# An S5 scan gated by a GeGLU feed-forward: token-major norm, one-pass GELU, pair-wide rotations and a fixed TensorE order

## The chip, the cores and the metric

The kernel runs on one core of a Trainium2 chip. The metric is the device time of one execution in microseconds (us). Every time below is a median of several executions. All are of the fast state, but for three executions of one kernel (c7), which are named. "Span" is the length of the one execution that was profiled; the times lie 1.6 to 1.9 us above it. Engines are called by the profile's names: PE is TensorE (PEld its weight loads), DVE is VectorE, ACT is ScalarE, POOL is GpSimd, SP is the engine that issues most transfers; a "q" behind a name is that engine's queue of DMA issues.

## The reference, cut to what matters

```python
x  = A_x                                    # (1, 2048, 512), bf16
xn = (x - mean(x)) / sqrt(var(x) + 1e-5)
# diagonal complex recurrence of 512 states
Lam_bar = exp(dt * Lam);  B_bar = ((Lam_bar - 1) / Lam)[:, None] * (B_re + 1j * B_im)
h[t] = Lam_bar * h[t-1] + B_bar @ xn[t]
s  = 2 * real(h @ (C_re + 1j * C_im).T) + xn * Dskip
# gate
g  = silu((gelu(xn @ w_gate) * (xn @ w_up)) @ w_down)        # 512 -> 1376 -> 512
out = x + s * g
```

The sequence is worked on in four slabs of 512 tokens. The complex recurrence becomes a real one by a rotation: the inputs are turned by a cosine and sine table, two real scans run with the factor |Lam_bar|, and the result is turned back.

## The kernel before

Three parts matter. The norm is channel-major: PE sums with a matrix of ones, ACT takes logarithm and exponential for 1/sqrt, and PE can do nothing else until it is through. The GELU has three ACT passes and two extra VectorE operations per tile:

```python
nc.scalar.activation(out=zb[:fs], in_=g_ps[:fs, :], func=AF.Copy)
nc.scalar.activation(out=sq[:fs], in_=g_ps[:fs, :], func=AF.Square, scale=math.sqrt(A_GELU))
nc.vector.scalar_tensor_tensor(out=arg[:fs], in0=sq[:fs], scalar=1.0, in1=zb[:fs], op0=ALU.add, op1=ALU.mult)
nc.scalar.activation(out=sg[:fs], in_=arg[:fs], func=AF.Sigmoid, scale=2.0 * C_GELU)
# ... up projection, Copy to ub; then zu = zb * ub and at = sg * zu on VectorE
```

The rotations work on one block of 128 states at a time: twelve `tensor_tensor` of 512 columns and two scans per block (cut):

```python
nc.vector.tensor_tensor(out=p1[:], in0=ure[:], in1=cos_b[:, pt, :], op=ALU.mult)
nc.vector.tensor_tensor(out=p2[:], in0=uim[:], in1=sin_b[:, pt, :], op=ALU.mult)
nc.vector.tensor_tensor(out=wre[:], in0=p1[:], in1=p2[:], op=ALU.add)
# ... the same for wim, two scans, carries, and six more to turn back
```

## Time and profile before

| before | value | how to read it |
|---|---|---|
| time | 266.82 us (266.12 to 267.13, 4 runs) | slowest core; there is one |
| span | 265.3 us | the profiled execution |
| busy PE / DVE / ACT | 195.9 / 228.3 / 157.4 us | sums of durations; they count overlap of pipelined work too |
| longest PE wait | 16.3 us, for the GELU's Square | ends at 58.59 us, where the body begins |

### The profile page before, as it was taken

The page shows a single profiled execution, that of the slowest core. Times are in us where ns is not written, and L with a number is a line of the kernel's source. Part 1 is how long each engine was busy: PE and PEld are TensorE (multiplying, and loading weights), DVE is VectorE, ACT ScalarE, POOL GpSimd, SP SyncE. Part 2 cuts the span into 40 slices and gives each one's busy share as a digit, 9 for nine tenths or more (in the row PEclk, how much of TensorE's full clock was granted, in tenths as well). Part 3 has the DMA queues.
Part 4 walks back from the last instruction along what each step waited for, and adds up shares of the span by engine and source line. Part 5 has one row for each costly group of instructions (what it writes and reads, how often), then busy time and mean ns, then how long its engine had stood idle before and what let it go on. Part 6 is the DMA issues. An engine that isn't in the chain of part 4 may idle for free.

```text
span 265.3 us, 2923 instructions
## 1 busy us (share of the span) xinstructions
PE 195.9 (74%) x863; PEld 86.3 (33%) x880; DVE 228.3 (86%) x600; ACT 157.4 (59%) x279; POOL 1.0 (0%) x8
## 2 busy tenths in 40 slices
PE   0045663019979889797795998789889788978993
PEld 0011221003434334343341443334444333434451
DVE  0405999987999999999999899999999999998243
ACT  0219999438747759748577527758475757922410
POOL 1000000000000000000000000000000000000000
PEclk9999759556999999999997999999999999999999
DMA  8999548100000000000000310000013000002201
GB/s 79 259 251 252 99 100 250 61 0 1 4 0 0 0 0 2 0 1 0 0 4 0 99 59 1 2 0 0 0 46 115 1 1 0 2 0 79 79 22 61
DMA packets 26224, 12.81 MB, mean 48 GB/s; under 512 B 19712, under 2 KB 25184, under 8 KB 26208
## 3 DMA queue, kind: packets, MB, share of 16 engines
q1 hardware_dynamic: 21520, 10.17, 15.8%
q10 hardware_dynamic: 4688, 2.46, 4.1%
q8 instruction: 7, 0.11, 0.2%
q14 instruction: 9, 0.07, 0.1%
HBM read 6.33 MB, written 2.10 MB: 32 GB/s over the span
## 4 chain that ended last, share of the span: by engine, by line
DVE 67%; PE 11%; ACT 9%; DMA 5%; issue 4%; SPq 2%; ACTq 1%; DVEq 0%
DVE fim L362 7%; DVE fre L359 7%; DVE arg L409 7%; DVE at L423 5%; DVE zu L422 5%; DMA xT<-in_A_x_dram 5%; PE y_ps L450 5%; PE f_ps L434 4%; DVE p L343 2%; DVE p L348 2%; DVE wre L344 2%; DVE p L349 2%; DVE hst L388 2%; DVE q L392 2%; DVE q L387 2%
## 5 line engine op out<-in xcount | busy, mean ns | idle before, releaser
L401 PE MATMUL g_ps<-xnT,wg 128*128 128x512 bf16 (+1 forms) x171 | 48.4, 399 | 32.7 <-ACT sq L407 28.5
L416 PE MATMUL u_ps<-xnT,wu 128*128 128x512 bf16 (+1 forms) x173 | 47.8, 396 | 6.3 <-ACT uim L338 5.9
L413 ACT ACTIVATE sg<-arg 128x512 bf16<-128x512 bf16 (+1 forms) x44 | 28.0, 636 | 34.0 <-DVE arg L409 34.0
L434 PE MATMUL f_ps<-wd,at 128*128 128x512 bf16 (+1 forms) x174 | 42.5, 379 | 3.5 <-ACT sf L440 2.2
L405 ACT ACTIVATE zb<-g_ps 128x512 bf16<-128x512 f32 (+1 forms) x44 | 26.6, 605 | 26.5 <-DVE zu L422 17.1
L401 PEld LDWEIGHTS <-wg 128*128 128x128 bf16 (+1 forms) x176 | 18.0, 103 | 53.0 <-issue 36.5
L450 PE MATMUL y_ps<-C,hst 128*128 128x512 bf16 x126 | 31.3, 379 | 1.3 <-DVE yg L462 0.8
L409 DVE SCALAR_TENSOR_TENSOR arg<-sq,zb 128x512 bf16<-128x512 bf16 (+1 forms) x44 | 29.9, 679 | 1.2 <-ACT sq L407 1.2
L416 PEld LDWEIGHTS <-wu 128*128 128x128 bf16 (+1 forms) x176 | 18.3, 104 | 29.6 <-issue 11.9
L420 ACT ACTIVATE ub<-u_ps 128x512 bf16<-128x512 f32 (+1 forms) x44 | 27.2, 618 | 0.0
L407 ACT ACTIVATE sq<-g_ps 128x512 bf16<-128x512 f32 (+1 forms) x44 | 26.8, 609 | 0.0
L434 PEld LDWEIGHTS <-at 128*128 128x128 bf16 (+1 forms) x176 | 17.0, 98 | 24.7 <-DVE at L423 2.3
L275 PE MATMUL mean_ps<-xT,onesK 128*128 128x512 bf16 x16 | 6.7, 563 | 19.1 <-DMA xT<-in_A_x_dram 17.2
L423 DVE TENSOR_TENSOR at<-sg,zu 128x512 bf16<-128x512 bf16 (+1 forms) x44 | 18.5, 421 | 1.5 <-ACT sg L413 1.5
L422 DVE TENSOR_TENSOR zu<-zb,ub 128x512 bf16<-128x512 bf16 (+1 forms) x44 | 18.4, 419 | 0.0
L462 DVE TENSOR_TENSOR yg<-y_ps,g 128x512 bf16<-128x512 f32 x16 | 10.7, 683 | 8.1 <-PE y_ps L454 7.8
L450 PEld LDWEIGHTS <-hst 128*128 128x128 bf16 x128 | 12.2, 98 | 14.9 <-issue 1.0
L325 PE MATMUL u_re_ps<-xnT,BreT 128*128 128x512 bf16 x62 | 16.1, 378 | 0.2
L331 PE MATMUL u_im_ps<-xnT,BimT 128*128 128x512 bf16 x61 | 16.1, 379 | 0.2
L438 ACT ACTIVATE fb<-f_ps 128x512 f32<-128x512 f32 x16 | 9.8, 613 | 9.7 <-PE f_ps L434 9.4
L359 DVE TENSOR_TENSOR_SCAN fre<-rho,init_re,wre 128x512 bf16<-128x512 f32 x12 | 15.3, 1279 | 0.0
L362 DVE TENSOR_TENSOR_SCAN fim<-rho,init_im,wim 128x512 bf16<-128x512 f32 x12 | 15.3, 1279 | 0.0
(119 smaller groups left out, 264.9 us busy)
## 6 DMA issues: line engine op xcount, KB each, us to landing
xres<-in_A_x_dram SPq DMA_DIRECT2D x16, 128.0 KB, 2.2
out_dram<-ot SPq DMA_DIRECT2D x16, 128.0 KB, 1.7
wu<-in_B_w_up_dram ACTq DMA_DIRECT2D x1, 1376.0 KB, 6.8
wg<-in_B_w_gate_dram SPq DMA_DIRECT2D x1, 1376.0 KB, 8.0
wd<-in_B_w_down_dram SPq DMA_DIRECT2D x1, 1280.0 KB, 6.9
wd<-in_B_w_down_dram SPq DMA_DIRECT2D x1, 96.0 KB, 6.6
BreT<-in_A_B_re_dram SPq DMA_TRANSPOSE x4, 6.0
BimT<-in_A_B_im_dram SPq DMA_TRANSPOSE x4, 2.7
```

Of the source, the lines that this page charges most:

```text
L359: nc.vector.tensor_tensor_scan(out=fre[:], data0=rho_b_ap, data1=wre[:], initial=ire, op0=ALU.mult, op1=ALU.add)
L362: nc.vector.tensor_tensor_scan(out=fim[:], data0=rho_b_ap, data1=wim[:], initial=iim, op0=ALU.mult, op1=ALU.add)
L401: nc.tensor.matmul(g_ps[:fs, :], lhsT=wg[:, kt, fsl], rhs=xnT[:, kt, cols], start=(kt == 0), stop=(kt == KT - 1))
L407: nc.scalar.activation(out=sq[:fs], in_=g_ps[:fs, :], func=AF.Square, scale=math.sqrt(A_GELU))
L409: nc.vector.scalar_tensor_tensor(out=arg[:fs], in0=sq[:fs], scalar=1.0, in1=zb[:fs], op0=ALU.add, op1=ALU.mult)
L413: nc.scalar.activation(out=sg[:fs], in_=arg[:fs], func=AF.Sigmoid, scale=2.0 * C_GELU)
L416: nc.tensor.matmul(u_ps[:fs, :], lhsT=wu[:, kt, fsl], rhs=xnT[:, kt, cols], start=(kt == 0), stop=(kt == KT - 1))
L420: nc.scalar.activation(out=ub[:fs], in_=u_ps[:fs, :], func=AF.Copy)
L422: nc.vector.tensor_tensor(out=zu[:fs], in0=zb[:fs], in1=ub[:fs], op=ALU.mult)
L423: nc.vector.tensor_tensor(out=at[:fs, j, :], in0=sg[:fs], in1=zu[:fs], op=ALU.mult)
L434: nc.tensor.matmul(f_ps[:, :], lhsT=at[:fs, k, m0 : m0 + P], rhs=wd[:fs, k, :], start=(k == 0), stop=(k == NFT - 1))
L450: nc.tensor.matmul(y_ps[:, :], lhsT=hst[:, j, m0 : m0 + P], rhs=C2[:, j, :], start=(j == 0), stop=False)
```

## The change

The intent: take work from VectorE until PE is the bound, and shorten the start. The diff cut to its core (cuts marked):

```diff
-  nc.scalar.activation(out=zb[:fs], in_=g_ps[:fs, :], func=AF.Copy)          # and sq, arg, sg, zu
+  nc.scalar.activation(out=gt[:fs], in_=g_ps[:fs, :], func=AF.Gelu_apprx_tanh)
+  nc.scalar.activation(out=ub[:fs], in_=u_ps[:fs, :], func=AF.Copy)
+  with tc.high_priority():
+      nc.vector.tensor_tensor(out=at[:fs, j, :], in0=gt[:fs], in1=ub[:fs], op=ALU.mult)
...
+  # norm on token-major tiles: bn_stats, bn_aggr, power on GpSimd, one tensor_scalar,
+  # then PE transposes (slab 0) or DMA transposes (slabs 1 to 3)
...
+  # rotation of a pair of blocks at once: 2 x 2048 columns and 2 x 1024
+  nc.vector.tensor_tensor(out=pp[:], in0=src[:], in1=cb, op=ALU.mult)
+  nc.vector.tensor_tensor(out=qq[:], in0=src[:], in1=sinp[:, :, hs, :], op=ALU.mult)
+  nc.vector.tensor_tensor(out=dst0, in0=pp[:, 0, :, :], in1=qq[:, 1, :, :], op=op)
+  nc.vector.tensor_tensor(out=dst1, in0=pp[:, 1, :, :], in1=qq[:, 0, :, :], op=op)
...
+  # cosine and sine tables by two long Sin passes; the input factor folded into C:
+  nc.scalar.activation(out=tA[:], in_=CT[:, 1, pt, :], func=AF.Copy, scale=cim[:, pt : pt + 1])
+  nc.vector.scalar_tensor_tensor(out=C2[:, 0, pt, :], in0=CT[:, 0, pt, :], scalar=cre[:, pt : pt + 1],
+                                 in1=tA[:], op0=ALU.mult, op1=ALU.subtract)
...
+  # silu by tanh, so that gate and GELU need no change of table set
+  nc.scalar.activation(out=th[:], in_=f_ps[:, :], func=AF.Tanh, scale=0.5)
+  nc.vector.scalar_tensor_tensor(out=g2[:], in0=th[:], scalar=1.0, in1=f_ps[:, :], op0=ALU.add, op1=ALU.mult)
...
+  # PE, ACT, SP and GpSimd keep the order of the program; VectorE's order is left to the compiler.
+  for s in range(NS):
+      # slab 0: FFN tiles first (with the fold of C on tiles 3 to 6), then the input matmuls, norms of 2 and 3
+      # later slabs: input matmuls, then FFN tiles, with the output y of slab s-1 after tiles 4, 6, 8, 10
+      # then the four down projections of slab s
```

## The prediction

> **What bounds the kernel now.** I read the page's busy row and slices first, then the busy time by stretches, the timeline of VectorE (DVE), the timeline of TensorE (PE), and the sums of waits.
>
> Parts 1 and 2 of the page, busy time and the 40 slices of 6.6 us:
>
> ```profile
> PE 195.9 (74%) x863; PEld 86.3 (33%) x880; DVE 228.3 (86%) x600; ACT 157.4 (59%) x279; POOL 1.0 (0%) x8
> ...
> PE   0045663019979889797795998789889788978993
> ...
> DVE  0405999987999999999999899999999999998243
> ```
>
> VectorE is full from slice 5 to slice 37; PE has work from slice 9 on and is not full. The busy time in three stretches, cut where the first and the last slab's feed-forward work lies (columns: stretch, its length, then busy us and instructions of PE, PEld, DVE, ACT, POOL):
>
> ```profile
> 0.00:57.40 57.40, 17.93 (x48) 6.20 (x49) 38.00 (x148) 31.10 (x38) 0.98 (x8) 0.82 0.72 156
> 57.40:245.00 187.60, 162.15 (x733) 72.63 (x748) 182.65 (x439) 121.94 (x233) 0.00 (x0) 0.97 0.05 15
> 245.00:265.30 20.30, 15.78 (x84) 7.52 (x84) 7.67 (x14) 4.34 (x8) 0.00 (x0) 1.00 0.16 53
> ```
>
> So there are three parts: a prologue of 57.4 us in which PE gets 48 matmuls, a body of 187.6 us in which DVE is busy for 97%, and a tail of 20 us that PE alone fills. A mean duration hides overlap, so I take costs from the distance between starts. In the VectorE timeline of the steady state (start, us, operation):
>
> ```profile
> 101.26 0.68 DVE L409 SCALAR_TENSOR_TENSOR arg<-sq,zb 128x512 bf16<-128x512 bf16 x1
> 101.89 0.42 DVE L423 TENSOR_TENSOR at<-sg,zu 96x512 bf16<-96x512 bf16 x1
> 102.23 0.41 DVE L422 TENSOR_TENSOR zu<-zb,ub 128x512 bf16<-128x512 bf16 x1
> 102.57 0.41 DVE L342 TENSOR_TENSOR p<-ure,cos_b 128x512 bf16<-128x512 bf16 x1
> ...
> 104.58 1.27 DVE L359 TENSOR_TENSOR_SCAN fre<-rho,init_re,wre 128x512 bf16<-128x512 f32 x1
> 105.77 0.39 DVE L350 TENSOR_TENSOR wim<-p,p 128x512 bf16<-128x512 bf16 x1
> ```
>
> A bf16 tensor_tensor of 512 columns costs 0.335 us (101.89 to 102.23 to 102.57), a scalar_tensor_tensor 0.60 to 0.63, a scan 1.19. The same distances in the table stage give 0.20 for 256 columns and 0.60 for 1024, so I extrapolate 1.13 us for 2048. Check, per slab: 11 feed-forward tiles x (0.60 + 0.335 + 0.335) = 14.0; four scan blocks x (12 x 0.335 + 2 x 1.19 + 0.4 for the carries) = 27.2; the gate and output work 4 x (0.60 + 0.60 + 0.335) = 6.1; together 47.3, and four slabs are 189 against the 187.6 of the body. VectorE's work is the body.
>
> The PE timeline where PE has no wait (start, us, operation and count):
>
> ```profile
> 105.11 1.03 PE L401 MATMUL g_ps<-xnT,wg 128*128 128x512 bf16 x4
> 105.98 1.03 PE L416 MATMUL u_ps<-xnT,wu 128*128 128x512 bf16 x4
> 106.84 1.03 PE L401 MATMUL g_ps<-xnT,wg 128*128 128x512 bf16 x4
> ```
>
> Four matmuls take 0.865 us, 0.2163 each, not the 0.379 to 0.401 of the groups. And in the sums of waits (total, times, longest), PE's waits stand behind the three-pass gelu:
>
> ```profile
> ACT sg L413 <- DVE arg L409: 34.0, 20, 4.2
> PE g_ps L401 <- ACT sq L407: 28.5, 12, 16.3
> ```
>
> **What the Trainium skill says.** (1) "TensorE: Matmul & The Clock Gate", section "Back-to-back issue gap": a warm matmul of N columns follows the last after N/2.4 + 2.5 ns, 216 for 512; this trace has 216.3. (2) The same page, Part 1: PE runs at half clock until some 3.4 us of activity, and again after an idle window. The body's granted clock of 0.97 and the prologue's 0.82 agree. (3) "VectorE: DVE Perf Modes", section "The perf-mode tier table": bf16 tensor_tensor in SBUF reaches 2x, single-source operations 4x in bf16 and 2x in fp32, PSUM sources less. The 0.335 us for 512 columns is 256 cycles plus about 0.07, so 2x is seen here; 4x on 512 columns is not seen here. (4) "ScalarE: Activation LUTs", section "What ACT_TABLE_LOAD costs": 1283 ns for a change of set; this trace has eleven loads of 1283 ns, eight of them in the old norm.
>
> **The change, part by part.**
> *Feed-forward.* The scalar_tensor_tensor and one tensor_tensor of each tile go: -0.94 us x 44 = -41 us of VectorE. ScalarE falls from four passes to two, about 0.49 us each by its starts, 1.0 us a tile beside 8 x 0.2163 = 1.73 of PE: PE no longer waits there.
> *Rotations.* One rotation over a pair of blocks costs 2 x 1.13 (2048 columns) + 2 x 0.60 (1024) = 3.46 instead of 2 x 6 x 0.335 = 4.02; a slab has four (two pairs, before and after the scan): 13.9 instead of 16.1. The scans stay, 8 x 1.19 = 9.5; carries about 1.0. With 11 x 0.335 = 3.7 for the gated product and 6.1 for the gate and output, VectorE needs 34.2 us a slab instead of 47.3.
> *PE a slab.* 196 matmuls of 512 (32 input, 88 feed-forward, 44 down, 32 output) x 0.2163 = 42.4, and 16 skip matmuls x 0.055 = 0.9: 43.3 us. That is above VectorE's 34.2, so **PE becomes the bound of the body**, and its total, 4 x 43.3 = 173.1 us, is what must be laid down. The old ones-matmuls of the norm go.
> *Prologue.* The order is fixed, so I walk it. Parameters land at about 5.5 (four issues of 0.5 us from 0.73, then 2 us), exp and two products until 6.8; statistics 4 x 0.6 + 0.6 (an estimate at one element a cycle) and the power on POOL until 10.5; four norms, PE transposes, four copies: xnT of slab 0 at 13.6 and PE starts. Then VectorE's tables: eight fp32 angle passes of 0.33 to 0.6, two fp32 passes over 2056 columns of 2.2 (2056 / 0.96 GHz), until 21 to 23; ScalarE's cosine takes 1.9 (as its 2048-column Square did), the small sines and a table load follow, and only then comes the first gelu, at 25 to 27, since ScalarE keeps program order. PE has by then done two tiles (16 matmuls) and stands with its four PSUM buffers full. **PE restarts at 26.5.** VectorE meanwhile does the coefficients (3.4) and the norm of slab 1 (5) and reaches the first gated product at 33; four buffers of gelu output and four of PSUM carry PE to about 35, so this costs little.
> *Stream.* 768 x 0.2163 + 3.5 = 169.6.
> *Losses on it.* Cold clock after the idle 2; folding C puts two ScalarE copies of about 0.7 on four tiles, where 2.4 exceeds 1.73: 2.6; slab 0's state against its first reader: VectorE from 33 has 46 us of work (norms of slabs 2 and 3 at 5 each, fold 5, products 5, gate 2.4, chains 24), so it is ready at 79, and PE wants it at 79: 2; other short waits 4.
> *Tail.* Output and skip matmuls, product, add, store: before, the last matmul ended at 260.9 of 265.3: 4.4.
> Sum: 26.5 + 169.6 + 2 + 2.6 + 2 + 4 + 4.4 = 211.1 us of span; times lie 1.6 above the span (266.9 against 265.3): **212 to 213 us**.
>
> **The rivals.**
> *A: VectorE stays the bound.* The cosine operand is now repeated by an outer step of zero. If that, or the four-dimensional pattern, loses the 2x rate in all four operations, a rotation costs about 6.7, a slab's four go from 13.9 to 27 and VectorE to 47, above PE's 43: 4 x 4 = 16 us more, about 228. For it: nothing in this trace has such an operand in a tensor_tensor. Against: the inner run is still dense, and the copies with a repeated inner element ran at 2x (1024 columns in 0.60).
> *B: the start costs more.* The norms of slabs 2 and 3 have high priority and their inputs arrive early, while VectorE's order in the body is left to the compiler. If they come before the first gated products, these move from 33 to 43 and PE, which can run to 35, stands for 8 us: about 220. For it: the page shows the first 57 us already lost to serial start-up. Against: VectorE has nothing else to do before slab 0's inputs arrive.
> *C: no start-up stall.* If the tables finish while PE still has free PSUM, PE runs through from 14: about 203. Against: ScalarE's two long sines alone take 3.8 us and wait for 4.4 us of fp32 passes.
> *D: late state.* If slab 0's state comes 10 us later than I count, PE waits as long at the first output matmul, about 220, and the clock drops for some us after.
>
> **Range and chances.** A and B each have perhaps one chance in six, C one in ten; most of the error is above the middle, as waits only add. I take 212, with 203 to 226. Even rival A with B, near 236, is 11% faster, and nothing I see costs 55 us. Faster 0.97, within 2% 0.02, slower 0.01.
>
> **What would show each step right or wrong.** Right: PE's slices at 9 from slice 6 on with few waits; VectorE's busy time near 185 us and gaps in the body; starts of the 2048-column rotations 1.13 apart; the first gated product near 33 us and the first gelu near 26; output matmuls that do not wait for the state. Wrong: rotations 2.2 apart (A); PE idle for over 5 us between 28 and 45 (B); a long PE wait for hst in slab 1 (D); the gelu and tanh taking turns of table loads between single tiles.

## The result, and the profile after

The changed kernel takes **227.01 us** (225.93 to 227.62, 4 runs) against 266.82: a ratio of 0.8503, 95% interval 0.8465 to 0.8541, faster. Ratios here are the mean time of one kernel's fast runs over that of the other's of the same rounds, so not quite the ratio of the medians. The direction was right; the time lies 1 us above the predicted range and 15 us above the predicted value.

The busy row and the slices of the page after (40 slices of 5.6 us):

```profile
PE 183.6 (82%) x849; PEld 84.6 (38%) x865; DVE 173.4 (77%) x315; ACT 95.1 (42%) x156; POOL 6.4 (3%) x13
...
PE   0018939069966999999829999999999999999993
...
DVE  1079869966899899999994279999932999995443
```

PE is full from slice 22 on (counted from 1), where the prediction had slice 6; before that it has holes. VectorE is full in the middle. The busy time in three stretches (columns as in the prediction: stretch, length, then busy us and instructions of PE, PEld, DVE, ACT, POOL, then granted clock):

```profile
18.60:60.00 41.40, 30.44 (x117) 12.79 (x119) 32.94 (x93) 27.87 (x45) 3.54 (x3) 0.88 0.55 122
60.00:117.00 57.00, 48.04 (x221) 21.83 (x224) 56.03 (x85) 21.14 (x36) 0.00 (x0) 0.94 0.06 14
117.00:220.00 103.00, 102.53 (x494) 48.01 (x502) 76.61 (x116) 43.06 (x72) 0.00 (x0) 0.98 0.04 15
```

From 117 us on PE is the bound, to within half a microsecond of 103. From 60 to 117 us VectorE is full, with 56.03 of 57.00; whether by the amount of its work or by its order is what the experiments ask. The prediction's "PE becomes the bound of the body" holds for the second half only.

PE's longest stops in its timeline (start of the work after the stop; in brackets the stop and what ended it):

```profile
31.39 1.54 PE L335 MATMUL up_ps<-xnT,wu 128*128 128x512 bf16 x4 [3.41 <-ACT ub L341]
45.90 1.87 PE L330 MATMUL g_ps<-xnT,wg 128*128 128x512 bf16 x4 [6.32 <-ACT gt L339]
68.93 6.60 PE L350 MATMUL f_ps<-wd,at 128*128 128x512 bf16 x22 [3.74 <-DVE g L357]
115.29 0.61 PE L350 MATMUL f_ps<-wd,at 128*128 128x512 bf16 x1 [4.11 <-DVE at L343]
```

With three shorter stops (0.37, 0.70 and 0.84) they make 19.5 us. After most of them the next matmuls are slow: the 22 after 68.93 took 6.60 us where 22 x 0.2163 is 4.76. From PE's start at 18.65 to its last matmul's end at 220.3 are 201.65 us; the whole stream at full rate is 4 x 43.3 = 173.1. So 28.5 us are lost, 19.5 in stops and 9 in slow matmuls and small gaps; of these 9, 1.4 come at PE's very start (eight matmuls in 3.12 us from 18.65).

Where the stops come from. The one at 45.90 is ACT waiting to fold C (ACT timeline):

```profile
41.20 0.72 ACT L257 ACTIVATE tA<-CT,cim 128x512 f32<-128x512 bf16 x1 [3.07 <-issue]
44.64 0.72 ACT L258 ACTIVATE tB<-CT,cim 128x512 f32<-128x512 bf16 x1 [2.71 <-DVE C L263]
45.27 0.58 ACT L339 ACTIVATE gt<-g_ps 128x512 bf16<-128x512 f32 x1
```

The fold's scratch has two buffers, and VectorE frees them late, because between 34.1 and 43.8 us it is mostly busy with the batch statistics of slabs 1 to 3. ACT keeps its order, so the GELU of the next tile stands behind the fold. The stops at 68.93 and 115.29 are VectorE's order (VectorE timeline, two pieces):

```profile
59.93 1.21 DVE L292 TENSOR_TENSOR pp<-U,cos_b 128x2048 bf16<-128x2048 bf16 x1
61.06 1.21 DVE L293 TENSOR_TENSOR qq<-U,sinp 128x2048 bf16<-128x2048 bf16 x1
...
63.52 4.56 DVE L306 TENSOR_TENSOR_SCAN Ft<-rho,Wt 128x512 bf16<-128x512 f32 x4
...
68.20 0.68 DVE L357 SCALAR_TENSOR_TENSOR g<-th,f_ps 128x512 f32<-128x512 f32 x1
...
110.10 2.46 DVE L306 TENSOR_TENSOR_SCAN Ft<-rho,it,Wt 128x512 bf16<-128x512 f32 x2
...
114.80 0.43 DVE L343 TENSOR_TENSOR at<-gt,ub 128x512 bf16<-128x512 bf16 x1
```

The gate at 68.20, which frees a down projection's PSUM bank, stands behind four scans, and the gated product at 114.80 behind two scans, an output product and a rotation, though ACT had delivered its inputs by 108 us. The first two lines show something else: the 2048-column rotations start 1.13 us apart (59.93 to 61.06), as extrapolated. Rival A is refuted.

The start (ACT timeline, queue of DMA issues and engine):

```profile
9.06 0.41 ACTq L88 DMA_DIRECT2D wu<-in_B_w_up_dram  x1
9.50 1.28 ACT L119 ACT_TABLE_LOAD   x1 [9.50 <-DMA wu<-in_B_w_up_dram]
10.79 0.21 ACT L119 ACTIVATE dt__124<-pf 128x4 f32<-128x4 f32 x1
```

The parameters had landed at 5.6 us, but the exponential stands behind six weight issues on ACT's queue, the last of which went out at 9.06. So PE began at 18.65 and not at 13.6.

### The profile page after: what moved, and what is told of

It reads as the page before. It is cut to its first block, busy times and chain, and to the rows that moved or that the text cites. A ratio compares the mean times of both kernels' runs of the same rounds, so it can differ in the third digit from the quotient of the medians.

```text
span 224.2 us, 2436 instructions
## 1 busy us (share of the span) xinstructions
PE 183.6 (82%) x849; PEld 84.6 (38%) x865; DVE 173.4 (77%) x315; ACT 95.1 (42%) x156; POOL 6.4 (3%) x13
## 4 chain that ended last, share of the span: by engine, by line
PE 49%; DVE 36%; DMA 8%; ACT 4%; POOL 1%; issue 1%; SPq 0%; DVEq 0%; POOLq 0%
PE f_ps L350 13%; PE g_ps L330 10%; PE up_ps L335 9%; PE y_ps L367 9%; DVE Ft L306 8%; PE u_ps L280 6%; DVE st L136 4%; DVE pp L292 4%; DVE qq L293 4%; DMA xnT<-xn 4%; DVE at L343 3%; DMA wu<-in_B_w_up_dram 2%; DMA pv<-in_A_log_dt_dram 2%; DVE xn L147 2%; PE y_ps L372 1%; POOL rs L142 1%
## 5 line engine op out<-in xcount | busy, mean ns | idle before, releaser
L335 PE MATMUL up_ps<-xnT,wu 128*128 128x512 bf16 (+1 forms) x174 | 46.8, 391 | 3.5 <-ACT ub L341 3.4
L339 ACT ACTIVATE gt<-g_ps 128x512 bf16<-128x512 f32 (+1 forms) x44 | 26.3, 597 | 33.8 <-PE g_ps L330 33.4
L341 ACT ACTIVATE ub<-up_ps 128x512 bf16<-128x512 f32 (+1 forms) x44 | 26.3, 598 | 11.8 <-PE up_ps L335 11.4
L306 DVE TENSOR_TENSOR_SCAN Ft<-rho,it,Wt 128x512 bf16<-128x512 f32 x24 | 29.6, 1273 | 0.0
L280 PE MATMUL u_ps<-xnT,BT 128*128 128x512 bf16 x124 | 28.1, 379 | 0.2
L357 DVE SCALAR_TENSOR_TENSOR g<-th,f_ps 128x512 f32<-128x512 f32 x16 | 11.0, 686 | 19.1 <-ACT th L354 19.1
L284 ACT ACTIVATE U<-u_ps 128x512 bf16<-128x512 f32 x32 | 19.1, 598 | 8.2 <-PE u_ps L280 8.2
L280 PEld LDWEIGHTS <-BT 128*128 128x128 bf16 x128 | 12.5, 98 | 15.1
L343 DVE TENSOR_TENSOR at<-gt,ub 128x512 bf16<-128x512 bf16 (+1 forms) x44 | 18.0, 416 | 0.0
L136 DVE BATCH_NORM_STATS2 st<-x_tok 128x6 f32<-128x512 bf16 x16 | 10.1, 684 | 0.0
```

The costliest lines, as they stand in the source:

```text
L136: nc.vector.bn_stats(out=st[:, m, :], in_=x_tok[:, s * M + m, :])
L280: nc.tensor.matmul(u_ps[:, :], lhsT=BT[:, ri, kt, pt * P : (pt + 1) * P], rhs=xnT[:, kt, cols], start=(kt == 0), stop=(kt == KT - 1),)
L284: nc.scalar.activation(out=U[:, ri, q, :], in_=u_ps[:, :], func=AF.Copy)
L306: nc.vector.tensor_tensor_scan(out=Ft[:, ri, q, :], data0=rho[:, pt : pt + 1].to_broadcast([P, TS]), data1=Wt[:, ri, q, :], initial=init, ...
L335: nc.tensor.matmul(u_ps[:fs, :], lhsT=wu[:, kt, fsl], rhs=xnT[:, kt, cols], start=(kt == 0), stop=(kt == KT - 1))
L339: nc.scalar.activation(out=gt[:fs], in_=g_ps[:fs, :], func=AF.Gelu_apprx_tanh)
```

## The experiments

Two theories stood at the outset, and the texts use these names. **Load**: VectorE has too much work before 117 us (tables, norms, fold, chains of slabs 0 and 1), and PE's stops are where that surfaces; a stop taken away comes back elsewhere. **Order**: the stops are separate accidents of the instruction order, and each one mended pays in full. A "chain" is rotation, scans, and rotation back of a pair of blocks. They ran in six calls, each on one chip and beside runs of the kernel before (medians 266.74 to 267.11); the chips differ between most calls (c4, c5 and c8 shared one, c6 had another), so times are compared across chips.

| run | us, median (range) | ratio to before, 95% | span |
|---|---|---|---|
| changed kernel | 227.01 (225.93–227.62) | 0.8503 [0.8465, 0.8541] | 224.2 |
| e1_fold4 | 225.37 (224.35–225.95) | 0.8425 [0.8372, 0.8478] | 224.2 |
| e2_norm_late | 222.54 (221.38–223.12) | 0.8326 [0.8280, 0.8373] | 219.6 |
| e3_exp_early | 223.70 (223.30–225.85) | 0.8392 [0.8336, 0.8448] | 221.4 |
| e4_rot_single | 231.22 (229.87–232.05) | 0.8652 [0.8601, 0.8703] | 228.1 |
| e5_gelu3 | 259.67 (257.55–260.97) | 0.9710 [0.9650, 0.9770] | 257.6 |
| e6_stats_shared (wrong on purpose) | 220.25 (219.23–220.67) | 0.8237 [0.8201, 0.8273] | 218.5 |
| e7_y_same | 252.04 (251.21–252.50) | 0.9429 [0.9382, 0.9475] | 250.2 |
| c2_combined | 221.01 (220.44–221.50) | 0.8270 [0.8237, 0.8304] | 219.4 |
| c4_uncoupled | 211.52 (211.35–212.87) | 0.7941 [0.7907, 0.7975] | 209.5 |
| c5_no_u_ahead | 211.21 (210.78–211.35) | 0.7911 [0.7892, 0.7930] | 209.5 |
| c6_weights_act | 219.85 (218.79–220.86) | 0.8249 [0.8203, 0.8295] | 217.4 |
| c7_dve_order | one fast run 213.43, three slow 217.11–218.68 | none | 216.9 (slow) |
| c8_dve_even | **206.98** (205.17–207.55) | 0.7750 [0.7694, 0.7806] | 204.9 |

### e1: the fold's stop taken away

```diff
-  tA = work.tile([P, D], FP32, name="tA", tag="tA")              # 2 buffers; tB alike
+  tA = work.tile([P, D], BF16, name="tA", tag="tA", bufs=4)
```

> The scratch of the folding of C gets four buffers instead of two (as bf16, for space). In the changed kernel TensorE stands 6.3 us at 39.4 us because ScalarE waits for this scratch. Theory 'order' (the three stalls are accidents of VectorE's order): this stall and about 1.6 us of cold clock after it go, 218 to 221 us. Theory 'load' (VectorE has too much to do before 117 us, and a stall that is taken away comes back at the gate or at the gated products): 225 to 228 us, with longer waits of TensorE at 65 and at 111 us.

The stop at 45.90 went (0.30 us is left there), and nearly all of it came back (PE timeline):

```profile
65.59 6.72 PE L350 MATMUL f_ps<-wd,at 128*128 128x512 bf16 x22 [5.76 <-DVE g L357]
...
113.09 4.46 PE L350 MATMUL f_ps<-wd,at 96*128 96x512 bf16 x12 [2.30 <-DVE at L343]
```

The gate's stop grew from 3.74 to 5.76, and a second gate stop of 1.98 us came; the two stops at the products are 2.04 and 2.30, where they were 4.11 and 0.84. The gain is 1.6 us, which is not clear of the noise: the intervals of the two ratios overlap, and both profiled spans are 224.2. As load said: PE came sooner to a VectorE that was not sooner.

### e2: the norms of slabs 2 and 3 a slab later

```diff
-            ln_dma(2)                    # after slab 0's input matmuls, at high priority
-            ln_dma(3)
+                if j == 0 and s < NS - 1:
+                    ln_dma(s + 1)        # in the slab before its use, without priority
```

> The norms of slabs 2 and 3 lose their high priority and are emitted one slab later (11 us of VectorE work, most of it moved behind the first slab's gated products). Theory 'load': the work moves towards the half in which VectorE has slack, so 217 to 220 us. Theory 'order': the stall at the fold goes as well, since nothing stands in front of the fold any more, so again 218 to 221; this run tells both from a third, that the early weight of the norms is harmless: 226 to 228.

222.54: the direction is right, the gain of 4.5 us is smaller than both theories said. The compiler still placed a part of the statistics early, and stops of 2.4, 2.0, 3.5 and 2.7 us remain.

### e3: the exponential ahead of four weight issues

```diff
+    nc.scalar.activation(out=rho[:], in_=a1[:], func=AF.Exp)
+    # weight loads 3 to 6 are issued here, after both exponentials, not before them
```

> The two exponentials of the parameters are issued on ScalarE ahead of the last four weight loads instead of behind all six. Expected: the first exponential at about 6.3 us instead of 10.8, TensorE's first feed-forward matmul at about 14.2 instead of 18.65. If VectorE's work bounds the time until 117 us ('load'), everything after it moves with it: 222 to 223 us. If the start is bound by the weights or by the transposed loads behind it, 226 to 227.

PE started at 13.80, 4.85 us sooner, and 3.3 us arrived at the end; 223.70 is 0.7 above what load said. The blocked queue had only moved: now the first GELU stood behind the last weight issue (ACT timeline):

```profile
18.87 0.52 ACTq L131 DMA_DIRECT2D wu<-in_B_w_up_dram  x1
19.42 1.28 ACT L343 ACT_TABLE_LOAD   x1 [12.84 <-DMA BT<-in_A_B_im_dram]
```

### e4: the pair-wide rotations undone

```diff
-        nc.vector.tensor_tensor(out=pp[:], in0=src[:], in1=cb, op=ALU.mult)     # 2048 columns
+        for q in range(H2):                                                     # 512 columns each
+            for ri in range(2):
+                TT(out=pp[:, ri, q, :], in0=src[:, ri, q, :], in1=cos_b[:, pt, :], op=ALU.mult)
```

> The pair-wide rotations are undone: 12 operations of 512 columns instead of 4 of 2048 and 1024, all else as in the changed kernel. VectorE gets 16 x 0.56 = 9 us more. If VectorE bounds nothing: 227. If it bounds the first two of four slabs only ('load'): half of it, 230 to 233. If it bounded the whole body: 236.

VectorE's busy time rose from 173.4 to 181.3, and the time by 4.2 us, about half. (PE also started later, at 19.89 for 18.65, which the edit does not explain.) That fits a kernel that VectorE bounds in its first half and PE in its second.

### e5: the three-pass GELU back

```diff
-        nc.scalar.activation(out=gt[:fs], in_=g_ps[:fs, :], func=AF.Gelu_apprx_tanh)
+        # Copy, Square, arg = (sq + 1) * zb, Sigmoid one tile later, zu = zb * ub, at = sg * zu
```

> The three-pass gelu of the kernel before goes back into the changed kernel (its last sigmoid, product and product a tile later, so that ScalarE's fixed order doesn't wait for VectorE): VectorE gets 44 x 0.94 = 41 us more and its work per slab, about 44.5 us, passes TensorE's 43.3. 'Load': VectorE then bounds the whole body, its busy sum of about 173 becomes 214 and the time 245 to 258 us. If the one-pass gelu mattered only in the first two slabs (half of 41): about 247 at most, and with VectorE idle in the second half; if it mattered little because TensorE bounds: below 235.

259.67, a little above the range. VectorE's busy time rose by 40.7 us to 214.1 (the prediction's term for this is 41). So 32.7 us of the 39.8 us that the change gains hang on this part.

### e6: the norm's statistics of slabs 1 to 3 left out (a wrong result on purpose)

```diff
-            mv, rs = ln_stats(s)
+            mv, rs = mv0, rs0            # slab 0's statistics; relative error 0.123
```

> Wrong result on purpose: slabs 1 to 3 are normalised with slab 0's mean and scale, so 12 batch statistics and 12 aggregates of VectorE, about 8.7 us, all before 60 us, are gone and nothing else moves. 'Load': the waits of TensorE at the fold, the gate and the gated product shrink by about as much in sum: 217 to 220 us. 'Order' without load: only the wait at the fold (6.3 and 1.6 of cold clock) changes: 219 to 221, with the waits at 65 and 111 us as they were. If neither: 226 to 228.

VectorE's busy time fell by 8.1 us (173.4 to 165.3; 8.7 were expected), and 6.8 us reached the end. 220.25 lies within what order said and 0.25 above what load said. The stops at the GELU and at the gate shrank to 2.62 and 1.48, against order; the one at the gated products stayed at 4.34, so this alone doesn't tell why it is there.

### e7: y in its own slab

```diff
-                if j in (4, 6, 8, 10):   # y of slab s-1 between the FFN tiles of slab s
+            for m in range(M):           # y of slab s right after its down projections
+                epi(s, m, y_mm(s, m, hsts[s]), g2s[s, m])
```

> The output matmuls of a slab stand after its own down projection again, not inside the next slab's feed-forward. VectorE's state for slab 0 is ready at about 87 us in the changed kernel, TensorE would ask for it at 76: 11 us of wait and some cold clock in slab 0, a few us in each later slab (state 38 us after the slab's start, asked for at 36): 240 to 248 us. If TensorE's order did not matter: 227.

252.04, worse than expected: PE waits for the state itself, once for 10.5 us (PE timeline):

```profile
88.63 2.74 PE L367 MATMUL y_ps<-C,hst 128*128 128x512 bf16 x6 [10.49 <-DVE hst L294]
```

Running y a slab late is thus worth 25 us. The effects of e4, e5 and e7 overlap: they sum to more than the whole gain.

### c2: the lessons combined

```diff
-        nc.scalar.dma_start(out=wg[:, :, a:b], in_=wg_r[:, :, a:b])
+        nc.sync.dma_start(out=wg[:, :, a:b], in_=wg_r[:, :, a:b])       # all weights by SP
+        nc.scalar.activation(out=fb[:], in_=f_ps[:, :], func=AF.Copy)   # the gate reads a copy, PSUM free sooner
+  # fold of C moved behind slab 0's down projections; norms as in e2; input matmuls of slabs 2, 3 a slab's downs earlier
```

> Several mends at once: all weight loads issued from the DMA queue that computes nothing, the folding of C after the down projections of slab 0, the norms of slabs 2 and 3 without priority, the gate's operand copied out of PSUM by ScalarE, and from slab 1 on the input matmuls of the next slab ahead of the down projection. Expected: TensorE starts near 14 us, no wait at the fold, the wait at the gate under 1 us, the wait at the gated products covered by the 6.9 us of input matmuls: 208 to 214 us under both theories if VectorE's order follows; 'load' says that slab 0 and 1 still show some waits, since 10 us of norm work still lie before 60 us.

Missed. PE started at 11.74 and had no stop of over 3.4 us until one of 18.59 us:

```profile
78.86 6.17 PE L279 MATMUL u_ps<-xnT,BT 128*128 128x512 bf16 x16 [18.59 <-ACT U L283]
```

The fold's ACT copies, with two buffers, now stood between the down projections and the evacuation of the next slab's inputs, and waited for VectorE. The coupling of ACT to VectorE had moved with the fold; it had not been removed.

### c4 and c5: the coupling removed

```diff
+        tA = work.tile([P, D], BF16, name="tA", tag="tA", bufs=4)       # tB alike
+        # the ACT half of the fold in the last four FFN tiles of slab 0, the VectorE half behind them
+        # slab 3's tokens are loaded in slab 1, so its norm cannot come early
-        # c5 only: input matmuls back at the head of their slab
         # for space, th becomes bf16 and g2 gets five buffers
```

> The combined version with the coupling taken out that stopped it for 18.59 us: the fold's ScalarE copies have four buffers each and stand in the last four tiles of slab 0's FFN, so that ScalarE never waits for VectorE's fold, and slab 3's tokens are loaded, and its norm done, a slab later. Load theory: VectorE was busy 39.93 of the 40 us from 60 to 100 us in the combined version, so its work still sets the pace there, and only a part of the 18.59 us comes back, some 6 to 12 us, with the norm of slab 3 (about 4 us) gone from the first half: 207 to 214 us, with TensorE waiting for VectorE in several smaller waits between 70 and 110 us. Order theory: the whole stall goes and nothing takes its place: 200 to 205 us. If the copies were not the cause at all: within 2 us of 221.

> The same as the uncoupled version, but with the input matmuls of each slab back at the head of their own slab, as the changed kernel has them, so that no chain is started a slab's down projections earlier. From 117 us on the TensorE was always fed in the changed kernel, so load theory expects no difference in the second half and at most 1 to 2 us in either direction from the uncoupled version. If starting the chains earlier is what feeds TensorE in slabs 2 and 3, this one is 3 us or more slower than the uncoupled version.

211.52 and 211.21: inside what load said, and no difference in time by the earlier input matmuls. But c4 did not get there by several smaller waits: it has no large stop at slab 1's products, and instead one that nobody expected, in slab 2. There ScalarE waited 9.63 us for a gate's buffers, since that gate stood on VectorE behind four scans of a chain that was started earlier (PE timeline of c4):

```profile
119.40 1.86 PE L335 MATMUL g_ps<-xnT,wg 128*128 128x512 bf16 x4 [7.33 <-ACT gt L344]
```

VectorE's busy time is 173.0 us in both, what it was in the changed kernel (173.4); the 15.8 us by which c5 is faster than that one came without taking work from VectorE. In c5 VectorE is still full in the middle (60 to 100 us), and PE stops at slab 1's gated products:

```profile
60.00:100.00 40.00, 31.62 (x153) 14.71 (x155) 39.90 (x63) 15.21 (x27) 0.00 (x0) 0.96 0.09 27
```

```profile
98.15 0.61 PE L355 MATMUL f_ps<-wd,at 128*128 128x512 bf16 x1 [4.41 <-DVE at L348]
101.03 10.40 PE L355 MATMUL f_ps<-wd,at 96*128 96x512 bf16 x34 [2.28 <-DVE at L348]
```

### c6: only the weight issues put back on ACT's queue

```diff
-        nc.sync.dma_start(out=wg[:, :, a:b], in_=wg_r[:, :, a:b])
+        nc.scalar.dma_start(out=wg[:, :, a:b], in_=wg_r[:, :, a:b])
```

> The version without chains started ahead (211.21 us), with one thing put back: the six weight loads are issued by ScalarE's queue again, as in the changed kernel. The exponential, and with it VectorE's statistics, norm and tables and the TensorE's first tile, should start 7 to 9 us later (18.7 to 20.7 instead of 11.67 us). Load theory: VectorE has next to no gap up to about 101 us in the version without this, so what it starts later it ends later, and the whole delay reaches the end: 217 to 220 us. Rival: the first half is paced by the order of waits and not by VectorE's total, so a later start is made up for by shorter waits, 211 to 214 us.

PE's first tile began 8.5 us later (20.18 for 11.67), and the time rose by 8.6 us, within what load said. Not all of it need be the queue's order: the parameters, too, landed 2.1 us later (PE's first work on them is at 5.51 for 3.36). The stops are the same, each about 8 us later:

```profile
106.13 0.61 PE L355 MATMUL f_ps<-wd,at 128*128 128x512 bf16 x1 [4.41 <-DVE at L348]
109.02 10.32 PE L355 MATMUL f_ps<-wd,at 96*128 96x512 bf16 x34 [2.28 <-DVE at L348]
```

### What the runs have in common

Put the moment at which PE takes slab 1's last gated product (the 96-row matmul, as at 101.03 above) beside the span:

| run | last product of slab 1 taken | span | difference |
|---|---|---|---|
| changed kernel | 116.74 | 224.2 | 107.5 |
| e2 / e3 / e4 / e6 | 111.54 / 114.25 / 120.78 / 111.38 | 219.6 / 221.4 / 228.1 / 218.5 | 108.1 / 107.2 / 107.3 / 107.1 |
| c5 / c6 | 101.03 / 109.02 | 209.5 / 217.4 | 108.5 / 108.4 |

The difference can be worked out: 34 down matmuls (7.35), two whole slabs (86.6), the third y (7.8), a cold clock (1.7) and the tail (3.9) make 107.4. So in these kernels the end is set when VectorE, in the order of its queue, comes to that product; what PE does before it only chooses where it stops. e1 is the exception in the set: 113.09, and then one more stop of 1.98 us for the gate. The runs that are not in the table stop PE later or give it another order. What was open: do the products come late because VectorE's total is too large, or because of what stands in front of them? In c5 slab 1's state was finished at 102.8 us, and PE wants it only after the rest of the down projections, the input matmuls and five FFN tiles of slab 2, some 20 us later (at 126.81). Scans that nobody waited for stood in front of products that PE waited for.

### c7 and c8: VectorE's order written by hand

```diff
-    ctx.enter_context(tc.manual_schedule(engines={ENG.PE, ENG.Activation, ENG.SP, ENG.Pool}))
+    ctx.enter_context(tc.manual_schedule(engines={ENG.PE, ENG.Activation, ENG.SP, ENG.Pool, ENG.DVE}))
+    # chains cut into pieces in a list; after every FFN tile so many pieces as fit, then the gated product
+    # c8: pieces counted with carry-over, the next norm in pieces ahead of the chains, chains carried
+    # into the next slab, and in the last slab y after all four down projections
```

> The version without chains started ahead (211.21 us), with the same instructions, but VectorE's order written by hand too: each gated product stands right behind its tile, with about 1.35 us of chain work between two of them, and the rest of a slab's chains goes between its down projections. There the last stops of TensorE were three waits for gated products of slab 1, 0.72 + 4.41 + 2.28 us, though slab 1's state, done at 102.78 us, is read only some 20 us later. Load theory in its strict form (VectorE's total before slab 1's state sets the pace): these stops go, but a stop of the same sum comes at the first output matmuls of slab 0 or of slab 1, or at the gated products, 208 to 212 us. Order theory (VectorE's total would suffice, the products only stand behind scans that nobody waits for yet): the three stops go, with the clock loss that follows them, and nothing takes their place: 200 to 204 us.

c7 is inconclusive. Three of its four runs were slow, the profiled one too, so its total says nothing; the fast one took 213.43. In the slow run's trace my hand order had put the norm and too much chain work among the products of slab 2 (stops of 3.36 and 1.68 us) and ahead of the output of slab 3 (3.15); stops of 1.34 and 2.23 us were left at slab 1's products.

> The hand-ordered version with the order mended: not more than about 1.3 us of chain work between two gated products of slab 1, the next slab's norm in pieces ahead of its chains, a part of the chains of each slab carried into the next one's input matmuls, and in the last slab the output matmuls after all down projections. Strict load theory: stops of 7 us or more in sum come back somewhere before the output matmuls of slab 1, 208 to 212 us. Order theory: at most 2 us of stops between 27 us and the output matmuls of slab 1, and 200 to 205 us, if slabs 2 and 3 stay without stops as they did before the hand ordering. If stops appear in slabs 2 and 3 alone, the time says nothing on the question, and the stops before 110 us decide.

c8 takes 206.98 us, the fastest of all. PE goes through slab 1's down projections without a stop (PE timeline):

```profile
91.47 9.68 PE L411 MATMUL f_ps<-wd,at 128*128 128x512 bf16 x43
```

VectorE's busy time is 175.5 us, not less than before. Between 27 us and the output matmuls of slab 1, PE's stops are 1.24, 1.38 and 1.63 us and three of 0.3: 5.2 us, where c5 has 10.0. That is more than the 2 that order allowed and less than the 7 of strict load, and the time, too, lies between the two forecasts (200 to 205, 208 to 212): neither was right in full. But the three stops of c5 at the products (7.4 us) are gone, and the largest that came in their place is 1.63; the granted clock rose from 0.967 to 0.992. PE reaches the first output matmul of slab 1 8.5 us sooner (first c8, then c5):

```profile
118.33 2.15 PE L430 MATMUL y_ps<-C,hst 128*128 128x512 bf16 x8
126.81 1.89 PE L374 MATMUL y_ps<-C,hst 128*128 128x512 bf16 x8
```

Of these 8.5 us, 3.9 are lost again in slabs 2 and 3, where c8 has stops of 1.22, 1.12 and 0.76 us and c5 has none. So **strict load falls**: up to slab 1's output, VectorE's total fits beside PE but for these small stops. What stays of it is that everything standing in front of a product in VectorE's queue, and a late start of that queue, was paid in full here (c6, c8).

Not tried: c8's order with the changed kernel's start, and c8 without its changed last slab; so what it loses in slabs 2 and 3 is not explained further. PE's first stop, of 3.40 us or more while ACT is at the Sin passes, is in every version, c8 included; no experiment took it away. PE's start also varies between kernels with the same start code (18.65 to 20.7 us with the weights on ACT's queue), which makes differences of 1 to 2 us between single traces uncertain.

## Why the prediction was right or wrong

The prediction's sum, with the measured terms in its place (start of the first tile, and losses beside the stream of 173.1, in us). "Measured" is by how much PE fell behind between those points, stops and slow clock together:

| term | predicted | measured |
|---|---|---|
| first tile starts | 13.6 | 18.65 |
| first stop, to the restart | 9.4 (26.5 − 13.6 − two tiles of 1.73) | 4.95 |
| fold and first gated products | 2.6 | 10.7 |
| gate and state of slab 0 | 2 | 5.6 |
| other waits and cold clock | 6 | 7.3 |
| stream | 173.1 | 173.1 |
| tail | 4.4 | 3.9 |
| span | 211.1 | 224.2 |

- **GELU, rotations, stream, tail: right.** Undoing the GELU puts 40.7 us on VectorE (41 predicted); rotations start 1.13 apart; the scan stayed at 1.2; PE's stream of 173.1 fits the second half, where PE has no stop at all after 117 us. VectorE's total was 173.4, where "near 185" was to be seen.
- **"PE restarts at 26.5": right in sum, by luck, through two errors.** I took the parameters at 5.5 as the start of the exponential and did not walk ACT's queue, where six issues stood in front. That cost 5 us. But the compiler had placed three GELUs ahead of the Sin passes, so PE had done four and a half tiles when it stopped, for 3.4 us. PE was then behind by 23.6 instead of 23.0. The signs named for this step failed: the first gelu came at 20.55, not near 26, and the first gated product at 24.02, not near 33.
- **"Losses on it", 10.6 in all, is the step that failed: 23.6 measured.** Within it the fold's 2.6 was worst: PE fell behind by 10.7 there. I costed the fold by its ACT copies alone; it couples ACT to VectorE through two buffers, and VectorE was in the statistics. The batch statistics came early, as rival B feared, but the three products among them (34.70 to 38.93) waited under 1 us each; the statistics hit through the fold. e1's four buffers and e6's missing statistics both shrink that stop (to 0.30 and 2.62 from 6.32), but mending it alone gained 1.6 us at most (e1), because PE then waited at the gates and products instead. "Other short waits 4" had no place for gates and products that stand behind scans.
- **The reasoning behind it: an average taken for a bound.** 34.2 us of VectorE a slab against 43.3 of PE says nothing on the first half, where VectorE also has tables, norms and fold. My own figures had the warning in them: slab 0's state at 79 us, and 34 us more for slab 1's work, is 113 us, if all of it stands in front of slab 1's last product; by my sum PE would have been at slab 1's last products at about 100 (13.6 + 9.4, 71.3 of stream, which is 173.1 less the 101.8 that is left there, and some 6 of losses). c8 shows the other half of it: ordered well, most of that work need not stand in front, so what failed was to count on a good order that nothing enforced.
- **Rivals.** A is refuted. B (about 220, by a stop of 8 us) happened in part: its sign, PE idle for over 5 us between 28 and 45, came (6.32 us before 45.90), but by the fold and not by late products. C is refuted by the stop at 31.39. D did not occur: PE did not wait for slab 0's state, which was ready at 87.1 us rather than 79, because PE itself came only at 90.9.
- **Cold clock.** I allowed 2 us once; about 9 us went in slow matmuls and small gaps, at PE's start and after several of the stops (granted clock 0.88 from 18.6 to 60 us, 0.98 from 117 us on). After the first stop alone it was 1.6 us (the twelve matmuls from 31.39), about what I allowed.

That the predicted 212 us is what nearly the same instructions give in a better order (211.21 in c5, 206.98 in c8; both have one ScalarE copy more at each gate) does not make the prediction right; it shows where the 15 us lay: 8.6 us in where the weights are issued (c6 to c5), about 7 us in the norms, the fold and the gate (changed kernel to c6, 227.01 to 219.85), which c6 mends together, so that these 7 are not divided.

## What to carry to other kernels

Before calling an engine the bound, add up each engine's work up to every point where the other waits for it, start-up included; an average per slab hides a full first half. In an in-order queue, what matters is what stands in front of the instruction that someone waits for: put the products that feed the bound engine first and fill in behind them with work whose reader comes later. And a scratch buffer shared between two in-order engines ties their queues together, so a stop there must be removed with more buffers, not moved.

## What the Trainium skill lacked or had wrong

- "DMA: Bandwidth & Descriptors", section "Issuing engines are not separate DMA queues", says that issuing on several engines saves only sequencer time, "usually small relative to the DMA itself". It does not say what the issues cost the engine that makes them: here six of them held ScalarE's first instruction until 9.50 us (11.03 in c6), and four of them, moved, its first GELU's table load until 19.42 us (e3). Putting them on SP made the kernel 8.6 us faster (c6 to c5).
- "VectorE: DVE Perf Modes", section "The perf-mode tier table", has no row for batch statistics or `scalar_tensor_tensor`. Here, from start to start: 0.60 us for the statistics of 512 columns, 0.60 for the gate's `scalar_tensor_tensor` of 512. Its 2x of `tensor_tensor` for 2048 columns is confirmed (1.22 us is the length of one), with an operand repeated by an outer step of zero too.
- "ScalarE: Activation LUTs", section "Table sets: the hidden batching unit", lists `gelu_apprx_tanh` only as separate from the set of `gelu`. Here it and `tanh` alternate without a load: four loads in the whole execution, none after 31.36 us.
